# One head's second weight load cut into strips and moved forward, and the result stored from another queue

## The chip, the cores and the metric

The kernel runs on one core of a Trainium2 chip. The metric is the device time of one execution in microseconds, 1309.87 as the median of three runs (1309.87 to 1310.05). Compute engines are TensorE (PE), VectorE (DVE), ScalarE (ACT) and GpSimd (POOL); SyncE (SP) issues nearly all loads. The loads are carried by 16 DMA engines.

## The reference

One token of a transformer block with a cache: layer norm, attention of 32 query heads over 8 cached key/value heads of 65536 positions, then a bilinear gated layer.

```
q = (layernorm(x) @ wq)                      # 1 x 512 @ 512 x 4096: 32 heads of 128
scores = q . k_cache / sqrt(128)             # 8 cached heads, each used by 4 query heads
o = softmax(scores) . v_cache                # 65536 positions a head, f32
h = x + o @ wo                               # 4096 x 512
y = h + ((hn @ w_gate) * (hn @ w_up)) @ w_down    # hn = layernorm(h), 512 -> 1792 -> 512
```

The two caches are 8 x 65536 x 128 x 4 bytes each, 268 MB; all weights together are some 28 MB.

## The kernel before

SBUF holds two buffers `kv[0]`, `kv[1]` of 128 partitions by 64 KB (8 MB each). For each of the 8 cached heads SyncE loads four chunks of K and four of V, each one load of 128 rows of 64 KB, into the two buffers in turn (line 148). Before each it waits until TensorE has finished with the chunk that lay in that buffer (line 133, `done[-2]`).

The weights of a head have one tile, `wqo_sb`, of 128 partitions by 16 KB: half is the query projection of the next head (`wq_sb`), half the output projection of this one (`wo_sb`). `wqo[h]` brings both in one load of 2 MB (line 138). It stands in the SyncE program at `i == NT + 2`, that is, ahead of the third V chunk, behind a wait for TensorE's Q step of the same head (`M_Q`), the last reader of the old `wq_sb`. Head 0's query weights come in a load of their own at the start (line 128). The semaphore `s_w` tells TensorE that the tile is there; it takes 16 from it ahead of the output projection (line 391).

TensorE runs a loop over the heads: Q, scores of four K chunks, transposes of the exponentials, four V chunks, output projection. After the loop comes the gated layer, whose weights `wg`, `wu` and `wd` are loaded into the freed `kv` buffers in cut pieces (lines 154 to 161). The last line of SyncE's program stores the result `y` when VectorE has copied it (lines 313 and 314), and waits for the landing.

Every instruction of an engine stands in the order in which the code issues it; nothing reorders it. A DMA is issued by the engine whose queue it is on, and the issue takes that engine's time, but not the transfer's.

Of the kernel before, what the change touches and what calls it, by code (L numbers as in the profile page):

```python
# [24 lines left out]
P = 128  # L25
# [12 lines left out]
LAST = HKV - 1  # L38
# [6 lines left out]
M_Q, M_K, M_MX, M_MB, M_T, M_L, M_V, M_PO, M_AT, M_HEAD = 1, 2, 6, 7, 8, 12, 13, 17, 18, 18  # L45
# [14 lines left out]
def body(nc, xc, xr, kT, v, wq0, wqo, wo7, wg, wu, wd, out):  # L60
    pe_e, dve_e, act_e, pool_e, sp = nc.tensor, nc.vector, nc.scalar, nc.gpsimd, nc.sync

    def tile(name, *shape, align=32):
        return nc.alloc_sbuf_tensor(name, list(shape), F32, align_bytes=align).ap()
# [17 lines left out]
    wqo_sb = tile("wqo_sb", P, 2, KT, 512, align=1024)  # L82
# [13 lines left out]
    g_sb, f_sb, y = tile("g_sb", P, FJ), tile("f_sb", P, FJ), tile("y", P, P)  # L96
# [8 lines left out]
    def sem(name):  # L105
        sems.append(nc.alloc_semaphore(name))
        return sems[-1]

    pe, dve, act, pool = (Counter(sem(n)) for n in ("pe", "dve", "act", "pool"))
    tok, atok = sem("tok"), sem("atok")  # L110
    s_kv = [sem("s_kv0"), sem("s_kv1")]
    s_wq, s_w = sem("s_wq"), sem("s_w")
    s_vp = [sem(f"s_vp{i}") for i in range(len(V_CUTS) - 1)]
    s_wg = sem("s_wg")
    s_wu = [sem(f"s_wu{i}") for i in range(len(U_CUTS) - 1)]
# [1 line left out]
    s_x, s_xr, s_out = sem("s_x"), sem("s_xr"), sem("s_out")  # L117
# [3 lines left out]
    def pe_at(h, m):  # L121
        return M_HEAD * h + m
# [7 lines left out]
    for h in range(HKV):  # L130
        for i in range(2 * NT):
            if len(done) >= 2:
                sp.wait_ge(pe.sem, done[-2])
            buf = len(done) % 2
            if i == NT + 2:
                sp.wait_ge(pe.sem, pe_at(h, M_Q))
                if h < LAST:
                    sp.dma_start(wqo_sb, wqo[h]).then_inc(s_w, 16)
                else:
                    sp.dma_start(wo_sb, wo7).then_inc(s_w, 16)  # L140
            if h == LAST and i == 2 * NT - 1:
                for p, (lo, hi) in enumerate(zip(V_CUTS, V_CUTS[1:])):
                    cs = slice(lo * 512, hi * 512)
                    sp.dma_start(kv[buf][:, cs], v[h, i - NT][:, cs]).then_inc(s_vp[p], 16)
            else:
                src = kT[h, i] if i < NT else v[h, i - NT]
                whole = i == 2 * NT - 1
                sp.dma_start(kv[buf], src).then_inc(s_vp[0] if whole else s_kv[buf], 16)
                for p in s_vp[1:] if whole else ():

                    sp.sem_inc(p, 16)
            done.append(pe_at(h, M_K + i if i < NT else M_V + i - NT))
    sp.wait_ge(pe.sem, pe_at(LAST, M_V + 2))
    sp.dma_start(wg_t, wg).then_inc(s_wg, 16)
    for p, (lo, hi) in enumerate(zip(U_CUTS, U_CUTS[1:])):
        cs = slice(lo * F, hi * F)
        sp.dma_start(wu_t[:, cs], wu[:, cs]).then_inc(s_wu[p], 16)
    sp.wait_ge(pe.sem, pe_at(LAST, M_V + 3))
    for p, (lo, hi) in enumerate(zip(D_CUTS, D_CUTS[1:])):
        cs = slice(lo * D, hi * D)  # L160
# [6 lines left out]
        out=ident, in_=ident, compare_op=ALU.not_equal, fill=1.0, base=0,  # L167
# [6 lines left out]
    def dve_self():  # L174
# [15 lines left out]
        out=xd, in0=x_col, scalar1=ln_m[:, 0:1], scalar2=None, op0=ALU.subtract))  # L190
# [10 lines left out]
        out=xn, in0=xd, scalar1=ln_r[:, 0:1], scalar2=None, op0=ALU.mult))  # L201
# [3 lines left out]
        out=sel_h, in_=ident.rearrange("p (g h) -> p h g", h=REP), axis=AX.X, op=ALU.add))  # L205
    dve.tick(dve_e.tensor_reduce(
        out=sel_b, in_=ident.rearrange("p (j c) -> p c j", j=4)[:, 0:16, :], axis=AX.X, op=ALU.add))
# [5 lines left out]
        out=neg_mean, in0=mean_m, scalar1=sel_1[:, 0:1], scalar2=-1.0, op0=ALU.mult, op1=ALU.mult))  # L213
# [7 lines left out]
    for h in range(HKV):  # L221
# [7 lines left out]
        for s in range(NT):  # L229
            dve_e.wait_ge(act.sem, copies[s])  # L230
            i = dve_e.tensor_reduce(out=mx[:, s:s + 1], in_=sc[s], axis=AX.X, op=ALU.max)  # L231
# [9 lines left out]
            out=mrow, in_=sm[1][0:1, 0:P].rearrange("p (g h) -> p h g", h=REP), axis=AX.X, op=ALU.max))  # L241
# [4 lines left out]
            out=nbias, in0=sm[0][:, 0:1], scalar1=-SCALE, scalar2=None, op0=ALU.mult))  # L246
# [6 lines left out]
        for s in range(NT):  # L253
# [7 lines left out]
            out=l4, in0=sel_h, scalar1=l1[:, 0:1], scalar2=None, op0=ALU.mult).then_inc(tok, 1)  # L261
# [7 lines left out]
            out=o_pad[:, :, 0], in0=sm[0][:, 0:REP], in1=linv, op=ALU.mult).then_inc(tok, 1)  # L269
# [12 lines left out]
        out=arow, in0=attn, scalar=1.0, in1=acc, op0=ALU.mult, op1=ALU.add, accum_out=rsum[:, 0:1]))  # L282
    dve_self()
    c_nmean = dve.tick(dve_e.tensor_scalar(
        out=nmean, in0=neg_mean, scalar1=rsum[:, 0:1], scalar2=None, op0=ALU.mult))
# [16 lines left out]
    for half in range(2):  # L302
        cs = slice(half * 256, min(FJ, half * 256 + 256))
        c_f.append(dve.tick(dve_e.scalar_tensor_tensor(
            out=f_sb[:, cs], in0=psc[0][:, cs], scalar=ln_r3[:, 0:1], in1=g_sb[:, cs],
# [4 lines left out]
    c_fp1 = dve.tick(dve_e.tensor_copy(f_pad[:, 8:NC, 0], sm[1][:, 0:6]))  # L310
    dve_e.wait_ge(pe.sem, T_D)
    c_y = dve.tick(dve_e.tensor_copy(y, pva[:, 0:P]))  # L312
    sp.wait_ge(dve.sem, c_y)
    sp.dma_start(out, y[0:P:32, :]).then_inc(s_out, 16)
    sp.wait_ge(s_out, 16)

    nums = [s.num for s in sems]
# [109 lines left out]
    for b in range(2):  # L427
        i = mm(sm[0][:, 4 * b:4 * b + 4], f_sb[:, b * P:(b + 1) * P], sel_q,
               start=(b == 0), stop=(b == 1))
# [10 lines left out]
    for c in range(NC):  # L440
# [4 lines left out]
        for j in range(4):  # L445
            o = c * D + j * P
            i = mm(pva[32 * j:32 * j + 32, 0:P], f_pad[:, c, :], wd_t[:, o:o + P],  # L447
                   start=False, stop=(c == NC - 1))
# [43 lines left out]
```

## Time and profile before

| | |
|---|---|
| Median of three runs | 1309.87 us |
| The profiled execution's own time | 1309.82 us |
| Its span, first to last instruction | 1308.5 us |
| TensorE, matmuls | 714.6 us, 55% |
| VectorE, ScalarE | 73.3 us, 47.3 us |
| Bytes read | 564.66 MB, 432 GB/s over the span |

The span runs from the first to the last instruction; the 1.3 us between it and the execution's time lie around it. Busy shares are over the whole span. DMA shares are of 16 engines together. "q1" is the queue of SyncE, "q10" that of ScalarE; "instruction" queues bring program code to the engines. A wait in a row stands with what ended it. In a view of DMA over a short stretch the stretch is cut into 40 equal slices: a digit is the busy share in tenths, and under it stand the GB/s of the packets that begin in that slice.

### The profile page before, as it was taken

To read this page: it belongs to the slowest core of one execution; us is meant where nothing else is said; L and a number is where in the kernel's file an instruction comes from. 1 tells how busy PE (TensorE), PEld (TensorE's weight loads), DVE (VectorE), ACT (ScalarE), POOL (GpSimd) and SP (SyncE) were. 2 spreads that over 40 slices of the span, in tenths; PEclk is the share of its full clock that TensorE was granted. 3 is DMA by queue.
4 is the path that set the end of the run, shared out by engine and by line. 5 is a ranking of instruction groups with operands and counts; after the bars stand their busy time and mean duration, and the time that the engine had idled before them with its cause. 6 is when DMAs were issued, how large, how long until landed. Compare 5 with 4: busy or idle time off the path is not lost. (4 is left out here: it accounts for less than half of the span.)

```text
span 1308.5 us, 10542 instructions
## 1 busy us (share of the span) xinstructions
PE 714.6 (55%) x4930; PEld 248.0 (19%) x4930; DVE 73.3 (6%) x180; ACT 47.3 (4%) x102; POOL 2.5 (0%) x13
## 2 busy tenths in 40 slices
PE   4355374562755547562564726636466455655557
PEld 3011031110312113120131202212022121311113
DVE  0000000100001000010000100001000010000101
ACT  0010000100001000010000100001000010000100
POOL 0000000000000000000000000000000000000000
PEclk9777676776776867786777777678677676677778
DMA  9999999999999999999999999999999999999998
GB/s 417 421 441 433 433 439 431 441 425 441 425 441 425 441 433 435 433 439 437 429 439 427 441 425 441 431 435 433 439 435 433 439 416 449 427 441 427 439 420 375
DMA packets 12404, 564.80 MB, mean 432 GB/s; under 512 B 1509, under 2 KB 1513, under 8 KB 2154
## 3 DMA queue, kind: packets, MB, share of 16 engines
q1 hardware_dynamic: 12248, 564.67, 99.7%
q8 instruction: 6, 0.10, 0.0%
q10 hardware_dynamic: 146, 0.00, 0.0%
q14 instruction: 4, 0.03, 0.0%
HBM read 564.66 MB, written 0.00 MB: 432 GB/s over the span
## 5 line engine op out<-in xcount | busy, mean ns | idle before, releaser
L353 PE MATMUL psc<-kv,q_pad 128*32 128x512 f32 x2048 | 294.5, 740 | 254.2 <-PEq L330 254.2
L381 PE MATMUL pva<-kv,pt 128*16 128x512 f32 x2048 | 282.0, 712 | 275.1 <-PEq L330 275.1
L353 PEld LDWEIGHTS psc<-kv,q_pad 128*32 128x32 f32 x2048 | 81.0, 133 | 461.1 <-issue 461.1
L381 PEld LDWEIGHTS pva<-kv,pt 128*16 128x16 f32 x2048 | 67.6, 111 | 492.3 <-issue 492.3
L225 ACT COPY sc<-psc 128x512 f32<-128x512 f32 x32 | 18.8, 587 | 1143.1 <-PE psc L353 1143.1
L231 DVE TENSOR_REDUCE mx<-sc 128x1 f32<-128x512 f32 x32 | 21.9, 686 | 536.1 <-ACT sc L225 536.1
L343 PEld LDWEIGHTS sm<-xn,wqo_sb 128*128 128x128 f32 x256 | 49.9, 303 | 10.4 <-issue 10.4
L343 PE MATMUL sm<-xn,wqo_sb 128*128 128x1 f32 x256 | 50.5, 332 | 2.2 <-issue 2.2
L265 DVE COPY orow<-pva 128x512 f32<-128x512 f32 x8 | 5.5, 692 | 567.0 <-PE pva L381 567.0
L368 PE MATMUL ptp<-ident,sc 128*128 128x128 f32 x128 | 29.0, 392 | 10.3 <-PEq L330 9.8
L368 PEld LDWEIGHTS ptp<-ident,sc 128*128 128x128 f32 x128 | 20.9, 198 | 15.9 <-issue 15.2
L250 ACT ACTIVATE sc<-sc,nbias 128x512 f32<-128x512 f32 x32 | 22.8, 713 | 20.0 <-DVE nbias L245 20.0
L255 DVE COPY pt<-ptp 128x512 f32<-128x512 f32 x32 | 22.1, 692 | 21.4 <-PE ptp L368 21.4
L394 PE MATMUL attn<-wqo_sb,o_pad 128*32 128x512 f32 x64 | 11.8, 813 | 3.4 <-PEq L330 3.4
L373 PE MATMUL pva<-zeros 128*32 128x512 f32 x64 | 12.9, 890 | 0.0
L388 PE MATMUL sm<-sel_b,orow 128*128 128x4 f32 x64 | 8.9, 262 | 7.2 <-PEq L330 7.2
L388 PEld LDWEIGHTS sm<-sel_b,orow 128*128 128x128 f32 x64 | 8.4, 205 | 14.4 <-issue 14.4
L359 PE MATMUL sm<-ident,m 128*1 128x128 f32 x8 | 2.2, 269 | 13.6 <-PEq L330 13.6
L371 PE MATMUL sm<-l,ones 128*128 128x4 f32 x16 | 3.8, 311 | 9.6 <-PEq L330 9.6
L416 PE MATMUL psc<-kv,hn_pad 128*32 128x448 f32 x64 | 8.0, 640 | 0.4 <-DVE hn_pad L287 0.3
L361 PE MATMUL sm<-ones,mexp 1*128 1x1 f32 x16 | 3.2, 267 | 5.7 <-PEq L330 5.7
L250 ACT ACTIVATION_READ_ACCUMULATOR sc<-sc,nbias 128x1 f32 x32 | 6.0, 189 | 0.0
(85 smaller groups left out, 64.4 us busy)
## 6 DMA issues: line engine op xcount, KB each, us to landing
wqo_sb<-in_wqo SPq DMA_DIRECT2D x7, 2048.0 KB, 13.9
kv<-in_v SPq DMA_DIRECT2D x1, 4096.0 KB, 21.3
kv<-in_wg SPq DMA_DIRECT2D x1, 3584.0 KB, 18.5
kv<-in_v SPq DMA_DIRECT2D x1, 2048.0 KB, 25.9
kv<-in_v SPq DMA_DIRECT2D x2, 1024.0 KB, 28.8
kv<-in_wu SPq DMA_DIRECT2D x1, 1792.0 KB, 22.6
kv<-in_wu SPq DMA_DIRECT2D x2, 896.0 KB, 25.1
kv<-in_wd SPq DMA_DIRECT2D x1, 1536.0 KB, 19.7
```

The lines of the kernel that those rows point to most:

```text
L225: copies.append(act.tick(act_e.copy(sc[s], psc[s % 2])))
L231: i = dve_e.tensor_reduce(out=mx[:, s:s + 1], in_=sc[s], axis=AX.X, op=ALU.max)
L250: act_e.activation(sc[s], sc[s], AF.Exp, bias=nbias[:, 0:1], scale=SCALE, accum_out=sums[:, s:s + 1]).then_inc(atok, 1)
L255: dve_e.tensor_copy(pt[s].rearrange("p g b h -> p b g h"), ptp[s % 2].rearrange("p (b g h) -> p b g h", b=4, h=REP)).then_inc(tok, 1)
L343: i = mm(sm[0][:, r:r + 1], wq_sb[:, k, r * P:(r + 1) * P], xn[:, k:k + 1], start=(k == 0), stop=(k == KT - 1))
L353: i = mm(psc[s % 2][32 * j:32 * j + 32, :], q_pad[:, 28 - 4 * rs:60 - 4 * rs], kv[s % 2][:, (4 * rs + j) * 512:(4 * rs + j + 1) * 512], st ...
L368: i = pe_e.transpose(ptp[s % 2][:, b * P:(b + 1) * P], sc[s][:, b * P:(b + 1) * P], ident)
L373: mm(pva[32 * j:32 * j + 32, :], zeros[:, 0:32], zeros, start=True, stop=False)
L381: i = mm(pva[32 * j:32 * j + 16, :], pt[n][:, 8 * j + rs, :, :].rearrange("p b h -> p (b h)"), vt[:, w * 512:(w + 1) * 512], start=False, ...
L388: i = mm(sm[0][:, 0:REP], orow[:, b * P:(b + 1) * P], sel_b[:, 4 * b:4 * b + 4], start=(b == 0), stop=(b == 3))
L394: i = mm(attn[32 * r:32 * r + 32, :], o_pad[:, r, :], wo_sb[:, r, :], start=True, stop=True)
L416: i = mm(acc[32 * j:32 * j + 32, :FJ], hn_pad[:, k, :], w[:, o:o + FJ], start=(k == 0), stop=(k == KT - 1))
```

## The change

Head 0's load of `wqo[0]` is taken from its place ahead of the third V chunk and issued right behind the third K chunk (`i == 2`). It is cut into 38 loads: the first 240 columns (960 bytes) of rows 0, 8, ... 120 in 15 strips of 16 columns (64 bytes), each strip in two loads, of r and of 16 - r rows, r from 1 to 15; the same 240 columns of the other rows in seven loads of 16 rows; and the remaining 3856 columns of all 128 rows in one load. All count on a new semaphore `s_st`. At the old place SyncE waits for the full count of `s_st` and adds 16 to `s_w` itself. The loads of the other heads are as they were. The store of the result goes from SyncE's queue to ScalarE's.

```diff
@@ semaphores
-    s_wq, s_w = sem("s_wq"), sem("s_w")
+    s_wq, s_w, s_st = sem("s_wq"), sem("s_w"), sem("s_st")
@@ ahead of the third V chunk
                 sp.wait_ge(pe.sem, pe_at(h, M_Q))
-                if h < LAST:
+                if h == 0:
+
+                    sp.wait_ge(s_st, n_st)
+                    sp.sem_inc(s_w, 16)
+                elif h < LAST:
                     sp.dma_start(wqo_sb, wqo[h]).then_inc(s_w, 16)
@@ behind the load of a chunk
+            if h == 0 and i == 2:
+
+
+                sp.wait_ge(pe.sem, pe_at(0, M_Q))
+                dst = wqo_sb.rearrange("p a k c -> p (a k c)")
+                src = wqo[0].rearrange("p a k c -> p (a k c)")
+                n_st = 0
+                for r in range(1, 16):
+                    cs = slice(16 * (r - 1), 16 * r)
+                    for rows in (slice(0, 8 * r, 8), slice(8 * r, P, 8)):
+                        sp.dma_start(dst[rows, cs], src[rows, cs]).then_inc(s_st, 16)
+                        n_st += 16
+                cs = slice(0, 16 * 15)
+                for k in range(1, 8):
+                    sp.dma_start(dst[k:P:8, cs], src[k:P:8, cs]).then_inc(s_st, 16)
+                    n_st += 16
+                sp.dma_start(dst[:, 16 * 15:], src[:, 16 * 15:]).then_inc(s_st, 16)
+                n_st += 16
@@ the end
-    sp.wait_ge(dve.sem, c_y)
-    sp.dma_start(out, y[0:P:32, :]).then_inc(s_out, 16)
+    act_e.wait_ge(dve.sem, c_y)
+    act_e.dma_start(out, y[0:P:32, :]).then_inc(s_out, 16)
     sp.wait_ge(s_out, 16)
```

SyncE's program at its start, before the change: a row is one DMA with its tile, its source and its shape, "x2" two alike in a row, and in brackets the semaphores that it waits for.

```order
L128 DMA wqo_sb<-in_wq 128x2048 [waits barrier_Pool_Activation_PE_DVE_SP_release]
L148 DMA kv<-in_kT 128x16384 x2
L148 DMA kv<-in_kT 128x16384 [waits pe] x2
L148 DMA kv<-in_v 128x16384 [waits pe] x2
L138 DMA wqo_sb<-in_wqo 128x4096 [waits pe]
L148 DMA kv<-in_v 128x16384
L148 DMA kv<-in_v 128x16384 [waits pe]
```

The weights stood there behind two chunks of V. After the change the same place of SyncE's program reads so, with the strips' first and last rows:

```order
L152 DMA kv<-in_kT 128x16384 [waits pe]
L166 DMA wqo_sb<-in_wqo 1x16 [waits pe]
L166 DMA wqo_sb<-in_wqo 15x16
L166 DMA wqo_sb<-in_wqo 2x16
...
L166 DMA wqo_sb<-in_wqo 1x16
L170 DMA wqo_sb<-in_wqo 16x240 x7
L172 DMA wqo_sb<-in_wqo 128x3856
L152 DMA kv<-in_kT 128x16384 [waits pe]
L152 DMA kv<-in_v 128x16384 [waits pe] x2
L152 DMA kv<-in_v 128x16384 [waits s_st,pe]
```

The 38 loads stand between the third and the fourth K chunk, and the third V chunk has the wait for `s_st` in front. The end of SyncE's program before:

```order
L161 DMA kv<-in_wd 128x3072 [waits pe]
L161 DMA kv<-in_wd 128x2048
L161 DMA kv<-in_wd 128x1024
L161 DMA kv<-in_wd 128x512 x2
L314 DMA out_y<-y 4x128 [waits dve]
L318 ISA [waits s_out]
```

After the change the store's row is gone from it and stands last in ScalarE's program, behind the gated layer's two activations:

```order
L272 ACTIVATE sc,sums<-sc,nbias 128x512 x3
L315 ACT_TABLE_LOAD
L315 ACTIVATE ln_t<-sm,eps_t 128x1 [waits pe]
L320 ACTIVATE g_sb<-psc,ln_r 128x448 [waits dve]
L336 DMA out_y<-y 4x128 [waits dve]
```

Only the store moved there; SyncE keeps the wait for its landing.

## Rows read from the trace of the kernel before

**Rows 1.** The page: busy time by engine (share) xinstructions; DMA queues: packets, MB, share

```profile
PE 714.6 (55%) x4930; PEld 248.0 (19%) x4930; DVE 73.3 (6%) x180; ACT 47.3 (4%) x102; POOL 2.5 (0%) x13
...
q1 hardware_dynamic: 12248, 564.67, 99.7%
q8 instruction: 6, 0.10, 0.0%
```

**Rows 2.** Windows of the stream of loads; the last number is GB/s

```profile
2.20:60.00 57.80, 26.49 (x164) 12.98 (x164) 4.14 (x17) 2.27 (x4) 1.04 (x4) 0.91 1.01 435
...
280.00:600.00 320.00, 172.23 (x1178) 58.82 (x1178) 17.00 (x38) 10.58 (x24) 0.00 (x0) 0.74 1.00 433
600.00:1270.00 670.00, 369.46 (x2484) 123.75 (x2484) 34.01 (x76) 22.43 (x49) 0.00 (x0) 0.71 1.00 434
```

**Rows 3.** The chain of waits, its end: start us, us, what

```profile
1283.09 22.80 DMA kv<-in_wd
...
1305.93 0.47 PE pva L447 x8
...
1306.42 0.29 DVE y L312
```

**Rows 4.** Waits of SyncE: for whom, us in total, times, longest

```profile
SPq L148 <- PE psc L353: 622.9, 32, 32.4
...
SPq L318 <- DMA out_y<-y: 1.1, 1, 1.1
```

**Rows 5.** Timeline of head 0: start us, us, what [idle before]

```profile
10.55 6.97 PE L343 MATMUL sm<-xn,wqo_sb 128*128 128x1 f32 x32 [2.19 <-issue]
...
34.54 0.33 SPq L148 DMA_DIRECT2D kv<-in_kT  x1
...
55.05 0.33 SPq L148 DMA_DIRECT2D kv<-in_kT  x1
...
84.59 8.56 PE L353 MATMUL psc<-kv,q_pad 128*32 128x512 f32 x64 [9.64 <-PEq L330]
...
111.21 0.44 SPq L148 DMA_DIRECT2D kv<-in_v  x1
```

**Rows 6.** Issues of wg and wd: ns min/median/max, first and last start

```profile
L154 SPq DMA_DIRECT2D kv<-in_wg x1: 328/328/328, 1270.1 to 1270.1; - x1
...
L161 SPq DMA_DIRECT2D kv<-in_wd x5: 328/432/433, 1281.3 to 1283.1; - x5
```

**Rows 7.** Issues of the small transfers, ns as in rows 6

```profile
L125 ACTq DMA_DIRECT2D x_col<-in_xc x1: 409/409/409, 0.7 to 0.7; - x1
L126 ACTq DMA_DIRECT2D x_row<-in_xr x1: 547/547/547, 1.2 to 1.2; - x1
L314 SPq DMA_DIRECT2D out_y<-y x1: 652/652/652, 1306.7 to 1306.7; - x1
```

**Rows 8.** The two issues in 30 to 60 us: mean us to landing

```profile
kv<-in_kT SPq DMA_DIRECT2D x2, 29.9
```

**Rows 9.** DMA queues in 0 to 20 us: packets, MB, share

```profile
q10 hardware_dynamic: 146, 0.00, 0.4%
```

**Rows 10.** GB/s by 75 ns from 50 and 1200 us; instruction queue, 30 to 60 us

```profile
GB/s 874 0 0 0 0 0 0 0 0 0 0 0 4369 2621 1748 874 1748 874 874 0 0 0 0 0 0 0 0 0 0 0 0 0 874 0 0 0 0 0 0 0
...
GB/s 0 0 0 0 0 0 0 0 0 1748 874 0 0 1748 2621 874 0 1748 0 0 0 874 0 0 0 0 0 874 874 874 874 0 0 0 0 0 0 0 0 0
...
q8 instruction: 1, 0.02, 0.2%
```

**Rows 11.** Timeline of TensorE's weight loads at the end

```profile
1305.29 0.16 PEld L447 LDWEIGHTS pva<-kv,f_pad 128*32 128x32 f32 x8 [0.23 <-DMA kv<-in_wd]
1305.92 0.16 PEld L447 LDWEIGHTS pva<-kv,f_pad 128*32 128x32 f32 x8 [0.47 <-DMA kv<-in_wd]
```

**Rows 12.** The page's DMA issues: KB, us to landing

```profile
kv<-in_wg SPq DMA_DIRECT2D x1, 3584.0 KB, 18.5
```

**Rows 13.** DMA share in tenths by 0.2 us from 1299 us

```profile
DMA  5999998999979799999999999953434110000000
```

## The prediction

> **What bounds the kernel now.** I read the busy shares first, then the rate by stretch, the chain of waits, SyncE's waits and only then single transfers. TensorE, the busiest compute engine, works 55% of the span, while the loads on SyncE's queue take 99.7% of the time of all 16 DMA engines [rows 1]. The rate is the same wherever one looks: 433 to 435 GB/s from the first load to 1270 us [rows 2]. A batch of 16 rows of 64 KB is 1.05 MB, so short stretches are uncertain by a batch at each edge (18 GB/s over 57.8 us, 1.6 GB/s over 670 us); 434 GB/s is what I work with, 27.1 GB/s for one of 16 engines. The chain that ended last is one load of `wd` queued behind everything else, then 0.47 us of TensorE and 0.29 us of VectorE [rows 3]; after that comes the store. SyncE spends nearly all its time waiting for TensorE to release a buffer, 32 times at L148 for K alone [rows 4]: it issues in time and the DMA engines never run dry. So the time is bytes over rate, plus some 2.2 us before the first byte and 2.6 us after the last. An edit counts only if it changes the bytes, the time that a DMA engine needs for them, the filling of the queue, or the two ends.
>
> **The load that moves.** The bytes are equal: 2 MB (2048 KB) in one load before, 2 MB in 38 loads after. It stood behind V's second chunk, now it stands behind K's third. K's fourth chunk and V's first two land 2,048 KB / 434 GB/s = 4.8 us later, and V's third when it did; TensorE waits for data in that stretch (the last K chunk's scores begin after 9.64 us idle [rows 5]), so it simply follows. Cost 0. The slack of the queue there: V's third chunk is issued at 111.21 [rows 5], and V's second chunk still has some 10 us to run (six loads of 8 MB and one of 1 MB from 2.2 us on, 51.4 MB at 434 GB/s, end at 120.6 us). Everything in this stretch moves by the same 4.8 us, so those 10 us stay, only without the weights as a further cover. The two waits added on SyncE are over when it comes to them: TensorE's Q step ended at 17.5 us [rows 5], and the strips land at about 70 us, 40 us before SyncE reaches the second wait. Behind that second wait stand V's third chunk and all that follows, but nothing waits: 0.
>
> **The issue of 38 loads on SyncE.** One issue takes 0.33 us for 128 full rows [rows 5], 0.43 in a series [rows 6], and 0.55 and 0.65 where a load has one row or four [rows 7]. That makes 38 x 0.33 = 12.5 us to 38 x 0.65 = 24.7 us from 34.9 us on, end at 47.4 to 59.6 us. Queued behind them is K's fourth chunk, issued at 55.05 us before [rows 5], so it may go out up to 4.5 us later. What hides this: the third K chunk is issued at 34.54 us and lands some 29.9 us later (the mean of it and the next [rows 8]), at 64.4 us, the first engines up to 1.5 us sooner (the lag of the late one at that time, below); then the strips' own 4.8 us follow. Cost 0. The cover is gone when one issue takes over (62.9 - 34.9) / 38 = 0.74 us; from there each 0.1 us costs 3.8 us.
>
> **The small packets.** These are what the trace of before bounds best, by the two loads of `x` on ScalarE's queue: 146 packets, nearly all of 16 bytes or completions, took 0.4% of 16 engines in 20 us [rows 9]. 0.004 x 16 x 20 us / 146 = 8.8 ns each. The 30 strip loads have 15 x 16 = 240 rows of 64 bytes, so 240 data packets and, with one completion for each engine used, 240 more: 480 x 8.8 ns = 4.2 us of engine time. The seven loads of 16 rows by 960 bytes add 7 x 32 x 8.8 ns = 2.0 us. Spread evenly this is 6.2 / 16 = 0.39 us on every engine, and as the DMA engines are what ends last, all of it shows. The ends: an engine with no strip pays 14 x 8.8 ns - 960 B / 27.1 GB/s = 0.09 us, one with a strip of every load 30 x 17.6 ns + 0.12 + 0.04 = 0.69 us. How rows are dealt to engines no row here shows. I take 0.39, nearest to the 8.8 ns measured and between the two.
>
> The Trainium skill (DMA: Bandwidth & Descriptors, "Why a DMA increments its semaphore by 16 and not by 1") says a load of r rows from this queue runs on the r lowest-numbered engines; by that the 30 strips are a ramp, two fewer on each next engine, and by it the term would be anywhere from 0.09 to 0.69 us, depending on which engine ends last. No run here shows it so far.
>
> The engines do not run in step, and which one is late matters: at 51 us 15 of them begin a row within seven slices of 75 ns and one comes 14 slices after them, 1 us; at 1200 us the starts spread over 22 slices, 1.6 us [rows 10]. An instruction fetch between 30 and 60 us took 0.2% of 16 engines there, 1 us of one engine [rows 10]; that is the likely source, and there are six such packets on that queue [rows 1]. They stay; SyncE's 37 added instructions may bring one more, on one engine out of 16, which I count at nothing (up to 1 us, if it is the last one).
>
> **The store.** SyncE's issue of it took 0.65 us; ScalarE's two issues took 0.41 (128 rows) and 0.55 us (one row) [rows 7]. ScalarE's work before it feeds the gated layer and ended long before TensorE's last step, so nothing stands in front, and SyncE's wait of 1.1 us for the landing is the same. I take the row nearest in shape, 0.55: -0.10 us. The ends are -0.24 (by the 0.41) and +0.14 (if what one row adds on ScalarE, 0.55 - 0.41, comes on top of SyncE's 0.65).
>
> **The sum.** +0.39 - 0.10 = +0.29 us on the profiled execution's 1309.82 (span 1308.5 and 1.3 around it); that lies 0.05 under the median 1309.87, so 1310.2 us. With the ends of both terms: 1309.7 to 1310.7. A measurement of this kernel tells about 0.2% (2.6 us) from no change; this is no change.
>
> **The rivals.**
> 1. *A bubble per load.* If an engine pauses at the border between two loads, 37 more borders count. The nearest rows are the last pieces of `wd`, 256 KB each: TensorE gets them at 1305.29 and 1305.92 [rows 11], 0.63 apart where 262,144 B / 434 GB/s = 0.60. 0.03 x 37 = 1.0 us: 1311.2. For: these borders have far less data between them to hide a pause. Against: 0.03 us is at the edge of what the rows resolve.
> 2. *SyncE can't queue that far ahead (slower).* The place is the end of the third K chunk. The most loads the trace shows outstanding are 9: at 1283.5 us `wg`, issued at 1270.07 and landing 18.5 us later, three of `wu`, five of `wd` [rows 6, 12], all issued without a stall. The change wants 39 to 40. If the queue takes only about 9, the other 30 are issued one by one after 62.9 us while the DMA engines idle, 30 x (0.33 to 0.65) = 10 to 20 us: about 1325. It decides from where fewer than some 38 may be outstanding, each missing place costs about 0.5 us. Against it: those nine have 9 x 128 rows, the 38 loads only 240 + 112 + 128.
> 3. *The engines end together (faster).* In the last 2 us the share of busy DMA engines falls 5 3 4 3 4 1 1 tenths in slices of 0.2 us [rows 13]: 2.1 slices of work over 7. If the delays put the engines in step, the end comes (7 - 2.1) x 0.2 = 1.0 us sooner, less the 0.10 of the store: 1308.7. Against: strips can only delay; the most that an engine is relieved of is 960 bytes, 35 ns, while the lag is over 1 us.
> 4. *Staggered rows flow faster.* If the 433 and 434 of the long stretches became the 435 of the first [rows 2], 320 x 2/435 + 670 x 1/435 = 3.0 us would go: 1306.8. Against: the stretch at 435 is the one in which the engines are most in step, and its edge is uncertain by far more.
> 5. *Each load pays its round trip in a row.* The store's landing was waited for 1.1 us after its issue [rows 4]; 37 x 1.1 = 41 us more, 1351. Against: the pieces of `wd` come 0.63 us apart [rows 11], bytes and all.
>
> On that last rival the Trainium skill (DMA: Bandwidth & Descriptors, "Anatomy of one DMA") gives a transfer a fixed 2.0 us, measured on another issue path; in a row that would be 37 x 2.0 us, 1384 us by its figure. The trace disagrees already at 0.63 us from one piece to the next.
>
> **How the numbers follow.** Forecast 0.68; bubble 0.12; queue full 0.06; together 0.08; flow 0.04; round trips in a row 0.02. The range reaches from rival 3 to beyond rival 1, 1308.6 to 1312.2, and leaves out the queue, the flow, the round trips and a little of the bubble's upper side. Over 0.2% slower (above 1312.5) are the queue, the round trips and 0.02 of the bubble: 0.10. Over 0.2% faster (below 1307.25) is the flow: 0.04. Within: 0.86.
>
> **What would show it.** In the new profile SyncE's strip issues end before 60 us, the fourth K chunk is issued before 62 us, the DMA share has no hole from 63 to 72 us, and the packet count rises by some 700. A hole there is rival 2 (with SyncE's issues stretched out past 65 us) or rival 1 (without). A last `wd` load that lands more than 1 us sooner, with a shorter decay of the DMA share, is rival 3. An issue over 0.74 us, or a time outside 1307.3 to 1312.5, proves the forecast wrong.

## The result, and the profile after

The changed kernel took 1314.35 us as the median of seven runs (1314.26 to 1314.85), the kernel before 1309.98, measured beside it (1309.87 to 1310.87). The ratio is 1.0033, with a 95% interval of 1.0021 to 1.0045: 4.4 us slower. The forecast was 1310.2 us and no change.

The page after shows how little of this a page tells; its lines on DMA packets and queues, as in [rows 1]:

```profile
DMA packets 13108, 564.80 MB, mean 430 GB/s; under 512 B 2101, under 2 KB 2217, under 8 KB 2858
...
q1 hardware_dynamic: 12944, 564.67, 99.7%
q8 instruction: 6, 0.10, 0.0%
```

The bytes, SyncE's share of the 16 DMA engines (99.7%) and the six instruction packets are as before. The packets are 13108 instead of 12404, 704 more, as forecast. The span is 1313.5 us instead of 1308.5; this execution is the longest of the seven.

Where the time went is read from the rate by stretch, as in [rows 2] (the last two numbers are DMA share and GB/s), with a short window on the place where the strips land:

```profile
2.20:60.00 57.80, 26.55 (x164) 13.04 (x164) 4.14 (x17) 2.27 (x4) 1.03 (x4) 0.91 1.01 433
62.00:74.00 12.00, 8.59 (x56) 2.54 (x60) 0.00 (x0) 0.00 (x0) 0.00 (x0) 0.64 1.04 311
280.00:600.00 320.00, 171.22 (x1178) 57.70 (x1178) 17.01 (x38) 10.54 (x24) 0.00 (x0) 0.73 1.00 434
600.00:1270.00 670.00, 362.44 (x2452) 122.63 (x2456) 34.03 (x76) 22.37 (x49) 0.00 (x0) 0.73 1.00 434
```

The same short window of the kernel before:

```profile
62.00:74.00 12.00, 8.72 (x60) 2.59 (x64) 0.00 (x0) 0.00 (x0) 0.00 (x0) 0.64 1.01 437
```

Ahead of the strips and from 280 us on the stream runs at 433 and 434 GB/s as before. From 62 to 74 us it is 311 instead of 437: 12 x 126 / 434 = 3.5 us worth of bytes are missing (a batch of 1.05 MB at an edge makes this uncertain by 2.4 us, so TensorE's starts below date the loss better). And the DMA share there is *higher* than before, 1.04: the packets that begin in these 12 us take, added up, more than 16 engines have time for. The short view of DMA in this stretch, 0.3 us to a slice, first before, then after:

```profile
DMA  5009950050099500500995005009950050099500
GB/s 218 0 0 1966 1092 218 0 0 218 0 0 1966 1092 218 0 0 218 0 0 1748 1311 218 0 0 218 0 0 1748 1311 218 0 0 218 0 0 1748 1311 218 0 0
```

```profile
DMA  0500079995949989989795959999989379999959
GB/s 0 218 0 0 4 59 163 267 74 62 78 55 215 215 215 264 264 212 370 212 463 206 411 206 514 527 694 694 424 373 476 154 308 758 643 758 707 540 218 437
DMA packets 889, 3.74 MB, mean 311 GB/s; under 512 B 624, under 2 KB 736, under 8 KB 736
```

In such a view a packet's whole time counts in the slice in which it begins, so a 0 is no idle engine: before, at 437 GB/s, 64 KB rows begin in bursts with zeros between them. After, almost nothing begins for three slices (the last rows of the third K chunk are under way), and from 63.5 to 67.4 us the rate is 55 to 267 GB/s while the digits are mostly at 7 to 9. As the sum of 1.04 says too, the engines are not idle between the 889 packets of the second view: many of them take long for their bytes. What kind of packet that is, is seen under f1.

TensorE dates the loss. Starts of groups of matmuls (start, length, [idle before]), before and then after: scores of the third K chunk, (after) of the fourth [rows 5], and the third V chunk, from which both kernels have loaded the same bytes:

```profile
65.28 9.68 PE L353 MATMUL psc<-kv,q_pad 128*32 128x512 f32 x64 [10.29 <-PEq L330]
...
147.25 9.64 PE L381 MATMUL pva<-kv,pt 128*16 128x512 f32 x64 [14.38 <-PEq L330]
```

```profile
65.41 9.70 PE L375 MATMUL psc<-kv,q_pad 128*32 128x512 f32 x64 [10.31 <-PEq L352]
93.94 9.09 PE L375 MATMUL psc<-kv,q_pad 128*32 128x512 f32 x64 [18.84 <-PEq L352]
...
151.70 9.21 PE L403 MATMUL pva<-kv,pt 128*16 128x512 f32 x64 [10.68 <-PEq L352]
```

The third K chunk is there at the same time. The fourth comes 93.94 - 84.59 = 9.35 us later, of which 4.8 were expected as position; the third V chunk comes 4.45 us later, and the median end 4.4. So nearly all of the loss arises between the third and the fourth K chunk, and stays to the end (this execution, 5.0 us longer, lost another 0.5 later on).

SyncE's issues in that stretch (start, length):

```profile
34.71 0.33 SPq L152 DMA_DIRECT2D kv<-in_kT  x1
35.08 22.22 SPq L166 DMA_DIRECT2D wqo_sb<-in_wqo  x30
57.35 5.54 SPq L170 DMA_DIRECT2D wqo_sb<-in_wqo  x7
62.93 0.58 SPq L172 DMA_DIRECT2D wqo_sb<-in_wqo  x1
63.57 0.42 SPq L152 DMA_DIRECT2D kv<-in_kT  x1
```

The 38 loads took until 63.5 us, and the fourth K chunk, issued at 55.05 before [rows 5], went out at 63.57. One issue of a strip, in ns min/median/max, against [rows 7]:

```profile
L166 SPq DMA_DIRECT2D wqo_sb<-in_wqo x30: 333/715/940, 35.1 to 56.9; - x30
```

The end is the same chain as in [rows 3], 5 us later, with the store now on ScalarE's queue (ACTq):

```profile
1310.32 0.16 PEld L469 LDWEIGHTS pva<-kv,f_pad 128*32 128x32 f32 x8 [0.28 <-DMA kv<-in_wd]
1310.95 0.16 PEld L469 LDWEIGHTS pva<-kv,f_pad 128*32 128x32 f32 x8 [0.47 <-DMA kv<-in_wd]
...
1311.44 0.29 DVE L334 COPY y<-pva 128x128 f32<-128x128 f32 x1 [6.15 <-PE pva L469]
1311.77 0.62 ACTq L336 DMA_DIRECT2D out_y<-y  x1
```

### The profile page after: what moved, and what is told of

It reads as the page before. It is cut to its first block, busy times and chain, and to the rows that moved or that the text cites. A ratio compares the mean times of both kernels' runs of the same rounds, so it can differ in the third digit from the quotient of the medians.

```text
span 1313.5 us, 10580 instructions
## 1 busy us (share of the span) xinstructions
PE 710.7 (54%) x4930; PEld 247.3 (19%) x4930; DVE 73.4 (6%) x180; ACT 47.2 (4%) x102; POOL 2.5 (0%) x13
## 2 busy tenths in 40 slices
DMA packets 13108, 564.80 MB, mean 430 GB/s; under 512 B 2101, under 2 KB 2217, under 8 KB 2858
## 3 DMA queue, kind: packets, MB, share of 16 engines
q1 hardware_dynamic: 12944, 564.67, 99.7%
## 5 line engine op out<-in xcount | busy, mean ns | idle before, releaser
L403 PE MATMUL pva<-kv,pt 128*16 128x512 f32 x2048 | 279.1, 705 | 271.4 <-PEq L352 271.4
L393 PEld LDWEIGHTS sm<-l,ones 128*128 128x128 f32 x16 | 3.6, 280 | 12.6 <-issue 12.6
```

The lines of the kernel that those rows point to most:

```text
L403: i = mm(pva[32 * j:32 * j + 16, :], pt[n][:, 8 * j + rs, :, :].rearrange("p b h -> p (b h)"), vt[:, w * 512:(w + 1) * 512], start=False, ...
```

## The experiments

Each kernel is the changed one with the block behind the third K chunk replaced as its diff shows, and with the store back on SyncE. Four theories went in. A: the short packets make an engine's reads fall behind. B: rows dealt 8 apart, 16 to a load, collide where they are written. C: the late issue of SyncE. D, which came up last: many small loads in a row cost by their number.

"K4" is the start of the scores of the fourth K chunk, the first milestone behind the loads, from each trace as above; "rate" is that of 62 to 74 us. Both are of one execution; that of e3 was the longest of its ten, 1310.85.

| run | loads in place of the 38 | us | ratio to before, 95% | K4 | rate |
|---|---|---|---|---|---|
| e1 | 1, whole | 1310.02 | 1.0000, 0.999 to 1.001 | 89.40 | 437 |
| e3 | 2, cut by columns | 1310.37 | 1.0003, 0.9993 to 1.0012 | 90.31 | 433 |
| e4 | 9 | 1310.56 | 1.0005, 0.9995 to 1.0015 | 90.32 | 433 |
| e10 | 5 | 1310.63 | 1.0005, 0.9991 to 1.0019 | 89.70 | 438 |
| e11 | 9, more packets | 1312.07 | 1.0016, 1.0002 to 1.003 | 90.69 | 389 |
| e12 | 23, even | 1313.05 | 1.0023, 1.0009 to 1.0037 | 92.84 | 346 |
| e8 | the change's 38 | 1314.31 | 1.0033, 1.002 to 1.0046 | 93.81 | 317 |
| e7 | 38, in two places | 1313.69 | 1.0028, 1.0017 to 1.0039 | 86.57 | 405 |
| e5 | 8, whole rows 8 apart | 1316.52 | 1.005, 1.0033 to 1.0067 | 95.81 | 262 |
| e6 | 38, no 960 bytes | 1317.57 | 1.0057, 1.0041 to 1.0074 | 97.52 | 214 |
| e9 | 8, 16 neighbouring rows | 1323.07 | 1.0101, 1.0084 to 1.0118 | 102.42 | 134 |
| f3 | 1 + 22 tiny, two at a time | 1310.28 | 1.0002, 0.9992 to 1.0012 | 89.48 | 437 |
| f4 | 11 tiny + 1 | 1311.12 | 1.0009, 0.9999 to 1.0018 | 91.01 | 394 |
| f1 | 22 tiny + 1 | 1313.18 | 1.0024, 1.0015 to 1.0034 | 93.08 | 342 |
| f2 | 38 tiny + 1 | 1316.18 | 1.0046, 1.0029 to 1.0062 | 96.29 | 221 |
| f5 | 22 of one row + 1 | 1311.34 | 1.001, 1.0001 to 1.002 | 90.98 | 432 |
| f6 | 38 tiny, the change's row counts, + 1 | 1314.80 | 1.0036, 1.0022 to 1.0051 | 94.24 | 308 |

The runs of before that go with them have medians of 1309.93 to 1310.03. The table's K4 is not to be compared for e7, which has only 18 of its loads ahead of that chunk; f3 has two of its 22 there.

### e1, e8: position and store

```diff
-                for r in range(1, 16): ... (38 loads)
+                sp.dma_start(dst[:, :], src[:, :]).then_inc(s_st, 16)
```

> Head 0's weights as one load of 128 rows by 16 KB behind the third K chunk; the store stays on SyncE. Three theories of the 4.4 us. A: the small packets themselves, an engine that meets a run of packets under 1 KB falls behind with its reads and shows their latency. B: the dealing of rows 8 apart, by which engines write into partitions that other engines write too. C: the issue, 0.72 us for each of 38 loads, so that the last loads reach the engines too late. All three expect no cost of the place: 1310.0, within 0.3.

Moving the load costs nothing: 1310.02 against 1309.96. Its fourth K chunk's scores give the time without any loss, 89.40:

```profile
89.40 9.35 PE L366 MATMUL psc<-kv,q_pad 128*32 128x512 f32 x64 [14.67 <-PEq L343]
```

e8 is the change with the store on SyncE alone:

```diff
-    act_e.dma_start(out, y[0:P:32, :]).then_inc(s_out, 16)
+    sp.dma_start(out, y[0:P:32, :]).then_inc(s_out, 16)
```

> The changed kernel with the store put back on SyncE. A, B and C: as the changed kernel within 0.3, 1314.1 to 1314.6; if the store's queue matters, the difference shows here.

1314.31 against 1314.35: the store's queue is worth less than the runs resolve. The 4.4 us are all in the cutting.

### e3, e4, e6: parts of the cutting

```diff
 e3
+                sp.dma_start(dst[:, 0:240], src[:, 0:240]).then_inc(s_st, 16)
+                sp.dma_start(dst[:, 240:], src[:, 240:]).then_inc(s_st, 16)
 e4
+                for k in range(0, 8):
+                    sp.dma_start(dst[k:P:8, 0:240], src[k:P:8, 0:240]).then_inc(s_st, 16)
+                sp.dma_start(dst[:, 240:], src[:, 240:]).then_inc(s_st, 16)
 e6: the 30 strips as they are, then
                 for k in range(1, 8):
-                    sp.dma_start(dst[k:P:8, cs], src[k:P:8, cs]).then_inc(s_st, 16)
+                    sp.dma_start(dst[k:P:8, :], src[k:P:8, :]).then_inc(s_st, 16)
-                sp.dma_start(dst[:, 240:], src[:, 240:]).then_inc(s_st, 16)
+                sp.dma_start(dst[0:P:8, 240:], src[0:P:8, 240:]).then_inc(s_st, 16)
```

> The load behind the third K chunk in two: 128 rows by 960 B and 128 rows by 15424 B; 2 issues, no rows 8 apart. A: eight packets of 960 B on each engine and the first long rows after them run slow as in the changed kernel, 1311 to 1312. B and C: 1310.0 to 1310.2 (eight more short packets an engine).

> No strips: eight loads of rows k, k+8, ... by 960 B, then 128 rows by 15424 B; 9 issues, done by 41 us. A: as with the 128-row form of the same bytes, 1311 to 1312. B: most of the loss, 1312.5 to 1314. C: 1310.2, since the issue is done 20 us ahead.

> The 30 strip loads stay, the other rows come as seven loads of 16 whole rows of 16 KB, rows 8 apart, and one of 16 rows by 15424 B; 38 issues. No packet of 960 B. A: the strips alone, 1311 to 1313. B: all rows are dealt 8 apart, so worse than the changed kernel, over 1314.4. C: as the changed kernel, about 1314.

Rows of 960 bytes by themselves, whether in one load or in eight, cost 0.4 and 0.6 us, within the intervals of the table. e6 was meant to take a suspect away and added another: its 16 KB rows in groups of 16, 8 apart, made it worse than the change.

### e5, e9: what groups of 16 rows do

```diff
+                for k in range(0, 8):
+                    sp.dma_start(dst[k:P:8, :], src[k:P:8, :]).then_inc(s_st, 16)        e5
+                    sp.dma_start(dst[16*k:16*k+16, :], src[16*k:16*k+16, :]).then_inc(s_st, 16)   e9
```

> Eight loads of 16 whole rows of 16 KB, rows 8 apart, behind the third K chunk; 9 issues, done by 41 us, no short packet. A and C: 1310.0 to 1310.4. B: the rows run at half rate, as they did beside the strips (about 1250 ns a row of 16 KB where 611 is usual), 4.9 us more: 1314 to 1315.5.

> Eight loads of 16 neighbouring rows of 16 KB. If rows 8 apart are slow because of where they lie in HBM, neighbouring rows are not: 1310.0 to 1310.5. If it is because several engines write partitions of one group, 16 neighbouring rows lie in fewer groups than 16 rows 8 apart: a quarter of the rate, 1310 + 3 x 4.9, 1322 to 1326. A and C: 1310.0 to 1310.4.

The windows from 62 to 74 us, e5 and then e9:

```profile
62.00:74.00 12.00, 7.16 (x44) 2.12 (x48) 0.00 (x0) 0.00 (x0) 0.00 (x0) 0.57 1.07 262
```

```profile
62.00:74.00 12.00, 4.61 (x24) 1.36 (x28) 0.00 (x0) 0.00 (x0) 0.00 (x0) 0.50 0.99 134
```

Theory B's slowdown exists: 262 and 134 GB/s against 437, at a DMA share of 1.07 and 0.99. At half the rate 2 MB cost 4.8 us more, at a quarter 14.5; measured are 6.5 and 13.1. The Trainium skill (SBUF — State Buffer, "Door 1: The DMA port swizzle") gives a map by which rows 8 apart reach half of the 16 ports and 16 neighbours a quarter; the runs agree with it; that the rows meet at these ports is not shown otherwise. But the strips and 960-byte rows hold only 120 KB, 0.28 us at the full rate and 0.55 at half: B cannot be the 4.4 us by bytes.

### e7: the late issue

```diff
+            if h == 0 and i in (2, 3):          # 18 strips behind the third K chunk,
+                for r in range(1, 10) if i == 2 else range(10, 16):   # the rest behind the fourth
```

> All 38 loads as in the changed kernel, with the same shapes in the same order, but the first 18 strip loads behind the third K chunk and the other 20 loads behind the fourth; the store on SyncE. Only the issue changes: each group is issued some 13 us after its chunk and 14 us before the DMA engines come to it. C (the last loads are issued too late): the loss goes, 1310.2 to 1310.8. A (short packets cost by themselves) and B (rows 8 apart): the loss stays, 1313.5 to 1314.5.

Here each load is issued well before its turn, and the fourth K chunk goes out at 54.40. The gain on e8 is 0.6 us. So the lateness of SyncE, the step that I had watched most closely, is at most that part (e7 also cuts the series in two).

### e10, e11: many short packets, few loads

```diff
+                for c in range(4):                 # e11: range(8)
+                    cs = slice(16 * c, 16 * c + 16)
+                    sp.dma_start(dst[:, cs], src[:, cs]).then_inc(s_st, 16)
+                sp.dma_start(dst[:, 64:], src[:, 64:]).then_inc(s_st, 16)
```

> The weights behind the third K chunk as four loads of 128 rows by 64 B and one of 128 rows by the rest; 5 issues, no rows 8 apart, every engine gets 4 x (8 + 1) = 36 short packets in a run. Theory A in a sharper form: while short packets run through an engine at 9 to 11 ns each, its reads fall behind, and the next long packets show the wait; it grows with the length of the run. A: 0.3 us for the packets and 1 to 2 us for the wait, 1311.3 to 1312.3. B (rows dealt to foreign partitions) and C (late issue): the packets alone, 1310.2 to 1310.5.

> As the run before with eight loads of 128 rows by 64 B: 72 short packets in a run on every engine, 9 issues. A: 0.7 us for the packets and 2 to 3.5 us for the wait, 1312.7 to 1314.2. B and C: 1310.5 to 1310.8.

Four loads of 128 rows bring each engine 36 short packets, and cost 0.6 us, within the noise; the K4 milestone is 0.3 us late, as 36 x 8.8 ns = 0.32. e11 with 72 has a wide interval, since another thing happens in it, in SyncE's issues:

```profile
34.78 17.52 SPq L165 DMA_DIRECT2D wqo_sb<-in_wqo  x8
52.35 9.64 SPq L167 DMA_DIRECT2D wqo_sb<-in_wqo  x1
62.03 0.43 SPq L152 DMA_DIRECT2D kv<-in_kT  x1
```

One of the eight loads and the one behind them held SyncE for 14 and 9.6 us. I read this as a queue that takes only so much ahead, rival 2's mechanism. Waiting were seven loads of 9 packets an engine (eight rows and a completion), the third K chunk's 9 and a few of the second: an estimate of some 80 an engine. A falls in its simple form: the number of packets is not the price.

### e12: 23 loads, evenly dealt, issued early

```diff
+                for r in range(15):
+                    cs = slice(16 * r, 16 * r + 16)
+                    sp.dma_start(dst[0:P:8, cs], src[0:P:8, cs]).then_inc(s_st, 16)
                 (the seven 960-byte loads and the rest as in the change)
```

> Each strip as one load of all 16 rows 0, 8, ... 120, so 15 strip loads with 15 packets and 15 completions on every engine in place of 0 to 30; the seven loads by 960 B and the rest as in the changed kernel; 23 issues, done by 50 us. A: a run of 44 short packets on every engine, 1311.5 to 1313. B: as the changed kernel, since the same bytes go to the same foreign partitions, 1313.5 to 1314.3. C: 1310.4.

+3.0 us with 22 small loads on every engine, all issued by 48.6 us, some 15 us before their turn. Neither the uneven strips nor the lateness is needed for most of the loss. Along e10, e4, e12, e8 K4 grows (89.70, 90.32, 92.84, 93.81) with the number of loads.

### e13: the same 38 loads on ScalarE's queue

```diff
-                        sp.dma_start(dst[rows, cs], src[rows, cs]).then_inc(s_st, 16)
+                        act_e.dma_start(dst[rows, cs], src[rows, cs]).then_inc(s_st, 16)
```

They stand behind ScalarE's copy of head 0's first scores, and GpSimd waits for `s_st` in SyncE's place.

> All 38 loads with their shapes issued on ScalarE's queue, behind its first copy of head 0 (about 35 us), so that the engines take them in turn with the 64 KB rows of SyncE's queue; SyncE's wait for them becomes one of GpSimd. A: no run of short packets any more, the loss goes, 1310.2 to 1310.8. B: the same bytes still cross, 1313 to 1314.5. C: the loss goes as in A.

Inconclusive on its question: three of four runs took 1331 to 1333 us, one 1312.66, and the ratio is 1.0092 with an interval from 1.002 to 1.0164. The profile is of one of the long runs, 1333.17 us; the short one has none. In it the K4 milestone is undisturbed (84.87), but the output projection waits:

```profile
205.11 1.93 PE L413 MATMUL attn<-wqo_sb,o_pad 128*32 128x512 f32 x8 [26.19 <-PEq L349]
```

The weights, issued by 61.7 us, were waited for until 205 us: 26 us too late. They trickled in between the rows of SyncE's queue; from 160 to 206 us the two queues still had this many packets:

```profile
q1 hardware_dynamic: 323, 18.02, 90.4%
q10 hardware_dynamic: 110, 0.78, 4.0%
```

Why one run of four was spared is open.

### f1 to f4: the number of loads alone

For D against B the small loads were taken out of the weights. The weights come whole as in e1, and ahead of them stand added loads of 16 rows by 64 bytes into a scratch tile that nobody reads:

```diff
+                for r in range(22):                # f2: 38, f4: 11
+                    cs = slice(16 * r, 16 * r + 16)
+                    sp.dma_start(scr[0:P:8, cs], src[0:P:8, cs]).then_inc(s_sc, 16)
                 sp.dma_start(dst[:, :], src[:, :]).then_inc(s_st, 16)
```

f3 has the 22 two at a time, behind each of 11 chunks.

> The weights come in one whole load behind the third K chunk (which cost nothing by itself), and ahead of it stand 22 added loads of 16 rows by 64 bytes into a scratch tile that nobody reads. Theory D (a series of many small loads costs by the number of loads in a row, whatever they carry): as 15 strips and seven loads of 960 bytes did, +2.5 to +3.0, 1312.5 to 1313.0. Theory B (the 960-byte loads, rows dealt 8 apart, are what falls behind; the 64-byte strips alone are only their 20 ns each): 22 x 0.020 = +0.4, 1310.4.

> As the run with 22 added loads, but 38 of them, as many loads as the change makes. Theory D: +4.4 as the change, 1314.4. Theory B: 38 x 0.020 = +0.8, 1310.8.

> The same 22 added loads of 16 rows by 64 bytes, two behind each of 11 chunks from the third K chunk on. Theory D (what costs is the series): two in a row never use up the queue's lead, 1310.0 to 1310.4. Rival (a flat price for each small load, 3.0 / 22 = 0.13 us): 1312.5 to 1313.0, as in a series. Theory B: 1310.4.

> 11 added loads of 16 rows by 64 bytes in a row. Theory D with a lead of some 18 loads, which the traces show at full speed: within it, 22 completions and packets, 1310.2 to 1310.6. A flat price of 0.13 us a load: 1311.4. Theory B: 1310.2.

Against 1309.93 of before: 11 cost 1.19 us, 22 cost 3.25, 38 cost 6.25, and 22 spread by twos 0.35. (The intervals of f4 and f3 reach no change; yet all ten runs of f4, from 1311.00, lie above all 25 of before, to 1310.34, which f3's do not.) The windows from 62 to 74 us of f1 and then f3, with the same 22 loads:

```profile
62.00:74.00 12.00, 8.76 (x60) 2.59 (x64) 0.00 (x0) 0.00 (x0) 0.00 (x0) 0.66 1.04 342
```

```profile
62.00:74.00 12.00, 8.69 (x56) 2.50 (x60) 0.00 (x0) 0.00 (x0) 0.00 (x0) 0.61 1.02 437
```

B falls: no 960-byte load, 22 KB in all, and more than 3 us. The flat price falls with f3, whose 0.35 / 22 = 16 ns a load is just two short packets of the 8.8 ns from [rows 9]. D's own forecasts held for f3 and nearly for f1, and missed twice: f2 (1316.18) is 1.8 us above its 1314.4, and f4 (1311.12) shows no lead of 18 loads that is free. In a row a load costs 0.11 us with 11 of them, and 0.19 each from the 11th to the 22nd, (3.25 - 1.19) / 11. (38 cost as much again for each, but there SyncE was held as in e11 and the weights went out at 64.42 us, so that part is not clean.) In f1 SyncE is not late: its loads' issues in ns, and how long they took to land:

```profile
L167 SPq DMA_DIRECT2D scr<-in_wqo x22: 579/589/653, 34.7 to 48.0; - x22
...
DMA to landing us min/median/max: 20.2/24.4/29.2
```

They were issued from 34.7 to 48.6 us and landed 20 us or more after their issue.

Where f1 loses its time is seen in a finer view, 62 to 68 us, 0.15 us to a slice:

```profile
DMA  9000000239999900009000000005799999950075
GB/s 437 0 0 0 0 0 2 13 17 363 363 247 562 221 0 0 4 5 111 0 0 0 0 0 0 0 0 218 328 546 437 328 328 546 437 109 0 0 328 218
```

From 62.9 to 63.35 us only small packets begin; then come the first 16 KB rows of the weights, 15 of them by 64.1 us and the last at 64.7. After that no packet begins on any engine until 66.1 us. So the small loads themselves run freely, and each engine then sits in its first long row for 2 us or more (the last one at least 1.3), where 16 KB at 27 GB/s want 0.6. In numbers: from 62.97 to 63.40 us 209 packets begin, all under 512 bytes, and the queue's row is

```profile
q1 hardware_dynamic: 209, 0.01, 30.0%
```

that is 0.30 x 16 x 0.43 us / 209 = 9.9 ns each, so that 22 loads of two packets take 0.44 us of the 3.25. The windows from 64.76 to 66.10 us of f1 and then f3:

```profile
64.76:66.10 1.34, 0.86 (x5) 0.26 (x9) 0.00 (x0) 0.00 (x0) 0.00 (x0) 0.50 0.00 0
```

```profile
64.76:66.10 1.34, 0.79 (x4) 0.23 (x8) 0.00 (x0) 0.00 (x0) 0.00 (x0) 0.50 0.97 416
```

The changed kernel's strips at first run as freely: from 63.35 to 63.66 us 190 packets under 512 bytes,

```profile
q1 hardware_dynamic: 190, 0.01, 38.3%
```

10 ns each. So theory A had the place right, the next longer packets, but not the measure: e10's 36 short packets an engine in four loads cost 0.6 us, f1's 44 in 22 loads 3.25. The price per load is an average; it is not paid between the loads.

### f5, f6: per engine, and the change's own row counts

```diff
 f5
-                    sp.dma_start(scr[0:P:8, cs], src[0:P:8, cs]).then_inc(s_sc, 16)
+                    sp.dma_start(scr[0:1, cs], src[0:1, cs]).then_inc(s_sc, 16)
 f6: 38 loads
+                    q = 8 * (r // 2 + 1) if r < 30 else P
+                    rows = slice(q, P, 8) if r < 30 and r % 2 else slice(0, q, 8)
+                    sp.dma_start(scr[rows, cs], src[rows, cs]).then_inc(s_sc, 16)
```

> The weights in one whole load behind the third K chunk, ahead of it 22 added loads of one row by 64 bytes into a scratch tile. If the price of a small load in a series (0.15 us a load with 22 of them on every engine) is paid by the engine that carries the row: one engine alone is 3.2 us later; the engines start up to 1.5 us apart, so the time is +1.7 to +3.2, 1311.7 to 1313.2, and the rate from 62 to 74 us falls by a sixteenth of what 22 loads of 16 rows took, from 437 to some 431 GB/s. If the price is paid in something that all engines share: +3.2, 1313.2, with the rate near 342 GB/s as there. If it needs packets on all engines: 1310.0 to 1310.4.

> The weights in one whole load, ahead of it 38 added loads of 64 bytes a row into a scratch tile, with the row counts of the change: 1 and 15, 2 and 14, ... 15 and 1 rows, then eight loads of 16. An engine gets 23 of them on average, the first one 38, the last ones eight. If the busiest engine sets the time: as with 38 loads of 16 rows, +6.2, 1316.2, less what the order of the engines gives back. If the mean does: 23 loads, +3.4, 1313.4. If only the small loads of the change matter, and not its 960-byte rows or its bytes, the time is the change's, 1314.3.

f5's rate from 62 to 74 us is 432, as for one engine of 16 being late (431), not 342 as when all are. Its time, +1.37, is below the 1.7 expected of one late engine. The trace gives the lead: 15 engines begin their last row of the third K chunk from 60.6 to 61.1 us and one at 62.1, and the small loads are not on that one, since their packets are through before its row ends. If the late engine sets the end of the kernel before, the engine with the 22 loads lost some 1.37 + 1.1 to 1.5 us, 2.5 to 2.9, an estimate; that a one-row load costs as much as one of 16 rows is not shown. The last 6 us of f5 show the late one, 0.15 us to a slice:

```profile
DMA  9954443442110000000000000000000000000000
GB/s 382 341 219 178 191 178 150 191 164 109 68 41 27 14 27 27 27 27 27 14 0 0 0 0 0 0 0 0 0 0 0 0 0 0 0 0 14 0 0 0
```

For the last eight slices, 1.2 us, the rate is 27 GB/s or less, that of one engine alone (the kernel before, below, is still at 68 in its last slice); read as the engine with the 22 loads, it carries its lag from 64 us to the end, 1240 us later. The rule of the Trainium skill that the forecast cites (DMA: Bandwidth & Descriptors, "Why a DMA increments its semaphore by 16 and not by 1"), r rows on the r lowest-numbered engines, agrees as far as this: 22 loads of one row all burden one engine. Which one it is no run shows.

f6 lost 4.8 us, the change 4.4. With nothing of the change but its row counts (and eight loads of 16 rows for its seven of 960 bytes and the rest) the loss is there: it lies between what f1 (22 loads on every engine) and f2 (38) lost, and 0.5 us above the nearest forecast, 1314.3. SyncE was as late here as in the change (the fourth K chunk went out at 63.82), so up to e7's 0.6 us of it may be lateness. The uneven dealing can be seen in the last 6 us of the kernel before and then after:

```profile
DMA  7989999998894344432100000000000000000000
GB/s 300 410 341 423 410 423 423 396 410 328 314 328 164 137 164 164 164 150 82 68 0 0 0 0 0 0 0 0 0 0 0 0 0 0 0 0 14 0 0 0
```

```profile
DMA  9745443443333321000000000000000000000000
GB/s 355 287 178 219 191 191 150 164 191 150 123 123 123 123 96 41 27 27 27 27 0 0 0 0 0 0 0 0 0 0 0 0 0 0 0 0 10 3 0 0
```

Before, the rate is below half for the last eight slices, 1.2 us; after, for 18, 2.7 us, and the last of them belong to one engine.

## Why the prediction was wrong, point by point

**The load that moves: 0.** Right (e1: 1310.02).

**The issue of 38 loads: 0.** Wrong in its size, and the smaller part of the loss. I took 0.33 to 0.65 us an issue from [rows 5 to 7]; a strip took 0.715 in the median and up to 0.94, and one of the seven loads behind them 1.78:

```profile
L170 SPq DMA_DIRECT2D wqo_sb<-in_wqo x7: 567/589/1781, 57.3 to 62.3; - x7
```

The cover that I had put at 0.74 us was just used up, (63.5 - 35.1) / 38 = 0.75; the fourth K chunk went out at 63.57, behind my limit of 62. With the issues spread (e7) 0.6 us came back, so this term was at most that instead of 0.

**The small packets: +0.39 us.** This is the step that failed. The 8.8 ns a packet were nearly right: 9.9 and 10 ns in f1 and the change. The step from there to the sum was not: that short packets cost an engine only their own time. Behind a series of small loads the next longer packets take long, and by how much goes with the number of loads, 0.11 to 0.19 us for each. With 22 loads on every engine f1 lost 3.25 us; the change has 22 to an engine on average, some engines more, and lost 4.4, where my term was 0.39.

**Rival 1, the bubble per load,** came nearest, with a chance of 0.12 and a price of 1.0 us: the loss does go by the number of loads. But in f1 there is no pause at the borders of the small loads; the wait comes in the long rows behind them. No row of the kernel before has a series of small loads, so none could price it. The price came from the last pieces of `wd`, 0.63 us apart with 0.60 us of bytes in them [rows 11]. I wrote that the strips' borders "have far less data between them to hide a pause" and then still multiplied the 0.03 us. A pause that lies beside 0.60 us of transfer shows only what exceeds it; the upper end should have been taken from a row with no bytes to hide it. The landing of the store, 1.1 us [rows 4], was one, used only in rival 5. Between 0.03 and 1.1 the rows left the price open, and my range knew only the lower end. The Trainium skill has a rule that speaks against this change and that I did not weigh (DMA: Bandwidth & Descriptors, "Bandwidth"): transfers under 64 KB are governed by their descriptors, and loads should be batched. The Trainium skill's figures there are for another issue path; here f1 bears the advice out for loads in a row (3.25 us for 22 KB), while in f3, by twos between 8 MB loads, batching would have saved no more than 0.35 us, their packets.

**Rival 2** (the queue full) did not decide here, though its mechanism exists (e11, f2). **Rival 3** went the other way: the engines end further apart. **Rivals 4 and 5** did not happen; 0.19 us a load is no round trip of 1.1.

**The store: -0.10.** 0.62 us on ScalarE instead of 0.65 [rows 7], so -0.03, and no difference in e8. Right in its direction, and too small to see.

**What would show it.** The packets (+704) came as said, and the fourth K chunk's issue, issues of up to 1.78 us and the time gave the contradiction. "No hole in the DMA share" was fulfilled (1.04) and meant nothing: a packet counts as busy while it waits. The sign that I had named for rival 1 could not have shown it; the GB/s beside it do.

What the long row waits for, and why the wait goes with the loads ahead of it and not with their packets, stays open. Reading ahead that falls behind during the series would fit the place of the wait, but no run here shows it, and none separates a small load from the completion packet that each brings with it.

## What to carry to other kernels

Where the DMA engines are the bound, count loads in a row, not bytes or packets alone: a 1 KB load behind others like it cost up to 0.19 us on each engine that carries it, paid in the next long packets, and by twos among large ones 0.016. A pause measured beside data that covers it is a lower bound and not a price. Read GB/s beside the DMA share, since an engine that waits inside a packet is shown as busy.

## What the runs showed of the hardware that was not expected

- Behind 22 small loads in a row, which ran at 9.9 ns a packet, no engine began a new packet for 1.34 us: all 16 were in one 16 KB row each (f1).
- Loads of 16 whole rows ran at 262 GB/s with the rows 8 apart (e5, +6.5 us) and 134 with neighbouring rows (e9, +13.1 us), in the 12 us around them, where one load of 128 rows ran at 437 (e1).
- SyncE was held for 13.85 us by the issue of one load in e11, and 4.8 us in f2, with some 80 packets an engine waiting in the queue by my count (an estimate).
- A one-row load was issued in 0.25 us in f5 (the median; 22 in 6.50 us with what lay between), a load of 16 rows by 64 bytes in 0.59, and the strips of other row counts in 0.72.
- The 38 loads on ScalarE's queue, beside SyncE's stream of 64 KB rows, were issued by 61.7 us and awaited until 205 us (e13, the profiled run; one other run of it was 20 us shorter).
